# Ten background items and the sums of h, dealt out anew over five w3 steps of an fp32 Fourier-mixing and MLP kernel

## The chip, the cores and the metric

One core of one Trainium2 chip runs the whole program in one launch. The metric is device time in microseconds, as a median of runs; lower is better. Engines are named as in the profile: PE (TensorE's matmuls), PEld (its weight loads), DVE (VectorE), ACT (ScalarE), POOL (GpSimd) and SP (SyncE, which issues every DMA of the stage told of here). Each engine works through its own instructions in the order in which the program issues them and waits for the other engines by semaphores.

## What is computed

The input is one sequence of 2048 rows with 512 features, all fp32. Two layers follow each other, and each has two sublayers, both with a residual:

```
x = x + real(DFT_seq(DFT_hidden(layernorm(x))))
x = x + B(layernorm(x))
B(x): h  = gelu(layernorm(x) @ w1), its four column groups shifted by +1, -1, +2, -2 rows
      x1 = x + shifted(h) @ w2
      return x1 + gelu(layernorm(x1) @ w3) @ w4        # 512 -> 1376 -> 512
```

The case is about the last line, the MLP with w3 and w4, in the second layer (layer 1 of 0 and 1).

## The kernel before

Every fp32 matrix product is made of three matmuls on fp32r parts (`mm3`, lines 294 to 296): a tile is split into a high part (a cast, mostly on ACT) and a low part (the difference, on DVE), and the products high*high, high*low and low*high are summed in PSUM. The rows are cut into four chunks of 512 (c = 0 to 3), a chunk into four tiles of 128 rows (q = 0 to 3).

The MLP takes two chunks at a time, a pair, and multiplies them block by block by Strassen's scheme with seven products in place of eight. In layer 1, pair 0 (chunks 0 and 1) is done by `first_pair` (line 1226) and pair 1 (chunks 2 and 3) by `last_pair`. Pair 0 runs while the layer norms of chunks 2 and 3 are still open, and does them beside its own work: it normalises and turns (transposes) them into z and writes z to DRAM (`z3d[2]`, `z3d[3]`), from where pair 1's blocks are read back.

`first_pair` has three parts.

1. Two products with the last block of w3 (`w4r[0]`), whose results go through gelu into `hm0` and `hm1`.
2. Five w3 steps, `p` = 0 to 4 (line 1330 on), which this text calls the first to the fifth. A step makes seven products (`prod`, six matmuls of 512 columns each) into five PSUM banks out of a round of eight. ACT copies the first (`u`, line 1356), DVE adds up the others (`v`, `x`, `y`, all through `add`, line 480), ACT takes gelus into the step's tiles `11`, `21`, `22`, `t3` (the `hn` tiles). The sixth product goes to a bank of its own; the fifth and the seventh add to the banks of the first and the fourth (`new=False`), so the fifth waits until ACT has copied `u`, and the seventh until DVE has added `y`.
3. Thirty-nine multiplications by blocks of w4 (`multiply`), each of 12 matmuls of 256 columns, with weights in seven tiles `un0` to `un6` that are loaded in a ring (`load`, line 1281) and lie where `w3b[1]` lay, the w3 blocks of the second and fourth steps. So the first seven loads can go when the fourth step's products are done. They are issued in the fifth step, after its second product.

Three kinds of work are dealt out between the products of the w3 steps.

- `bg` is a list of ten items (`z3_steps`, line 1027), taken one by one by `one()`. Counted from 0, they are: 0 and 1, the low parts of blocks `t3` and `t4`; 2, statistics of two tiles of chunk 3 (DVE, POOL) and the norm of two tiles of chunk 2 (ACT); 3, the same for the other two; 4, DVE turns two tiles of chunk 2 into `z3turned`; 5, it turns the other two, and SP issues four DMAs that write `z3d[2]` (`turn_out`, line 614); 6 and 7, DVE adds two tiles of chunk 3 to `xs`, and ACT norms them; 8 and 9, as 4 and 5, for chunk 3 and `z3d[3]`.
- `t_sum(k, i)`: four DVE sums (Strassen's sums of h) for each step k, with i from 0 to 3; the sums of steps 0 to 3 are dealt out over steps 1 to 4 by the table `sums` and, within a step, over its four points `then(0)` to `then(3)`. `then(1)` stands between the additions `x` and `y`; `then(2)` and `then(3)` stand after the fifth and the sixth product's gelu; an item that is taken at a point follows the point's sums.
- `bring(a, b)` (line 1353): SP reads blocks a to b of the w3 step two steps on, in three pieces, after the fourth, sixth and seventh product.

Items are taken at three kinds of places: after the first and after the head products and in the first step's beginning (items 0 and 1), at points of a step by the condition in `then`, and at the end of the first three steps (`if p < 3: one()`, after `bring(3, 4)`).

In the fifth step `then` also splits the first tiles for part 3 (`high_at` on ACT, `low_at` on DVE), and the four loads `b12f`, `b11f`, `b21f`, `b22f` (line 707) read z of chunks 2 and 3 back; three of them stand in SP's queue behind the seven `un` loads, the fourth after the second multiplication.

Of the kernel before, what the change touches and what calls it, by code (L numbers as in the profile page):

```python
# [43 lines left out]
def spectral_mlp_kernel(ctx: ExitStack, tc: tile.TileContext, x, ws, hs, w1, w2, w34, out):  # L44
# [105 lines left out]
    def piece(src, a=0, b=2):  # L150
        pieces.append((src, a, b))
        return len(pieces) - 1
# [9 lines left out]
    for layer in range(LAYERS):  # L162
        for c in range(NC):
# [5 lines left out]
            for k in range(NP):  # L169
# [4 lines left out]
                p = piece(ws[c, k][:, 2:4])  # L174
# [18 lines left out]
    raws, slots, sums = {}, {}, {}  # L193
# [285 lines left out]
    def add(o, a, b, op=ALU.add):  # L479
        nc.vector.tensor_tensor(o, a, b, op=op)  # L480
# [145 lines left out]
    def gelu(g, ps):  # L626
        order = "p (q b j) -> p b q j", "p (b q j) -> p b q j"
        g_of, ps_of = (v.rearrange(o, b=NB, q=TC) for v, o in zip((g, ps), order))
        nc.scalar.activation(g_of, ps_of, AF.Gelu_apprx_tanh)
# [83 lines left out]
    def prod(o, w, u, b, new=True):  # L713
        for d in range(2):
            v = slice(d * P, (d + 1) * P)
            mm3(o, w[:, 0, u, v], w[:, 1, u, v], blk[b][:, d, 0], blk[b][:, d, 1], new and d == 0, d == 1, not new)
# [7 lines left out]
    def by_pairs(layer, zs, xin, dst):  # L724
# [347 lines left out]
        for pair in range(n_pairs):  # L1072
            c1, c2 = 2 * pair, 2 * pair + 1
            if last_of(layer):
                if pair == n_pairs - 1:
                    last_pair(c1, c2, dst, lambda: w4r[0])
                    continue
                loads = [next_block(*b) for b in ((3, 0, "12"), (2, 0, "11"), (2, 1, "21"), (3, 1, "22"))]
                first_pair(c1, c2, dst, z3_steps, loads, next_parts, w3_load, w3e_load)
                continue  # L1080
# [145 lines left out]
    def first_pair(c1, c2, dst, z3_steps, loads, next_parts, w3_load, w3e_load):  # L1226
# [15 lines left out]
        def one():  # L1242
            if bg:
                bg.pop(0)()

        def t_sum(k, i):
            f = {n: v[1] for n, v in parts[k].items()}
            o, a, b = (("t1", "t3", "11"), ("t3", "22", "t3"), ("t2", "22", "t1"), ("t4", "21", "t2"))[i]
            add(f[o], f[a], f[b], ALU.subtract)
# [29 lines left out]
        def load(n):  # L1279
            if n < len(steps):  # L1280
                nc.sync.dma_start(units[n % len(units)].bitcast(F32), steps[n][2])
# [4 lines left out]
        def high_at(i):  # L1286
            if i < len(ring):
                k, n = steps[ring[i]][1]
                act(hi_of(ring[i]), parts[k][n][1])

        def low_at(i):
            if i < len(ring):
                k, n = steps[ring[i]][1]
                lo, src = parts[k][n]
                nc.vector.tensor_tensor(lo, src, hi_of(ring[i]).bitcast(F32), op=ALU.subtract)
# [18 lines left out]
        for i, pair_of in enumerate((("11", "21"), ("12", "22"))):  # L1314
            s = w4r[0]
            for d in range(KD):
                b = blk[pair_of[d // 2]]
# [8 lines left out]
        u, v = (at(f"uv{i}", TMP + (4 + i) * CH, CH, dtype=F32) for i in range(2))  # L1326
        x, y = rest[4:6]
        sums = [(k, i) for k in range(nk - 1) for i in range(4)]
        sums = {p: sums[a:b] for p, a, b in ((1, 0, 2), (2, 2, 6), (3, 6, 12), (4, 12, 16))}
        for p in range(nk):  # L1330
            w = w3b[p % 2]
            b1, b6, b7, b5, b4 = (banks[(2 + 5 * p + i) % 8] for i in range(5))
            f = {n: t[1] for n, t in parts[p].items()}
            last = p == nk - 1

            todo = sums.get(p, [])

            def then(i):
                for k, n in todo[len(todo) * i // 4 : len(todo) * (i + 1) // 4]:
                    t_sum(k, n)  # L1340
                if last:
                    high_at(i)
                    if i:
                        low_at(i - 1)
                elif p and i > (0, 1, 1, 2)[p]:
                    one()

            def gelu_to(n, ps):
                gelu(f[n], ps)

            def bring(*v):
                if p + 2 < nk:
                    nc.sync.dma_start(w[:, :, slice(*v)].bitcast(F32), w3d[p + 2][:, :, slice(*v)])

            prod(b1, w, 4, "11")
            act(u, b1)
            prod(b6, w, 1, "t2")
            add(v, u, b6)
            if not p:
                one()  # L1360
            then(0)
            if last:
                for n in range(len(units)):
                    load(n)
            prod(b7, w, 2, "t3")
            add(x, v, b7)
            then(1)
            prod(b5, w, 0, "t1")
            bring(0, 3)
            add(y, x, b5)  # L1370
            gelu_to("22", y)
            prod(b1, w, 5, "21", new=False)
            gelu_to("11", b1)
            then(2)
            if last:
                for f_ in loads[:2]:
                    f_()
            prod(b4, w, 6, "t4")
            bring(4, 7)
            add(x, x, b4)  # L1380
            gelu_to("21", x)
            then(3)
            if last:
                loads[2]()
            prod(b5, w, 3, "22", new=False)
            add(v, v, b5)
            gelu_to("t3", v)
            bring(3, 4)
            if p < 3:
                one()  # L1390
# [6 lines left out]
        for n in range(len(steps)):  # L1397
# [4 lines left out]
            if 10 <= n < 31 and n % 3 == 1:  # L1402
                i = (n - 10) // 3
# [528 lines left out]
```

## Time and profile before

| | |
|---|---|
| median of 3 runs | 1425.03 us (1424.76 to 1426.95) |
| the profiled execution's own time | 1425.46 us |
| its span, first to last instruction | 1423.4 us |
| PE busy | 1416.0 us (99%) |
| DVE busy | 1187.3 us (83%) |
| ACT busy | 741.2 us (52%) |
| granted clock of TensorE | 1.000 |

The span leaves 2.06 us of the profiled execution's time outside. Times in timelines count from the span's start. A row of a timeline gives start, duration, engine, line, operation, out<-in, shapes and count; a bracket at its end gives the engine's idle time before it and what ended it.

The five w3 steps of `first_pair` begin on PE at 1207.23, 1216.75, 1226.27, 1235.79 and 1245.31 us, 9.52 us each, and its part 3 lies after them, up to about 1313 us.

### The profile page before, as it was taken

What the parts mean: (1) busy time and instruction counts of PE and PEld (TensorE: products, weight loads), DVE (VectorE), ACT (ScalarE), POOL (GpSimd) and SP (SyncE); (2) the same over time, 40 slices, a digit from 0 to 9 for tenths busy, and PEclk for the clock granted to TensorE, in tenths of its full rate; (3) what the DMA queues carried; (4) which work ended last, traced back from release to release, by engine and by line L of the source; (5) the groups of instructions that cost most, each with busy time, mean ns of one, the idle gap of its engine ahead of it and who ended that gap; (6) DMA issues with size and microseconds to landing.
All of it is one profiled execution on the core that took longest, in us unless ns stands there. A gap on an engine that the chain in (4) does not pass through costs nothing.

```text
span 1423.4 us, 17862 instructions
## 1 busy us (share of the span) xinstructions
PE 1416.0 (99%) x6465; PEld 1181.6 (83%) x6465; DVE 1187.3 (83%) x1675; ACT 741.2 (52%) x1007; POOL 77.2 (5%) x105
## 2 busy tenths in 40 slices
PE   9999999999999999999999999999999999999998
PEld 8888888888888888888888888888888888889887
DVE  7986998988979888656789989889899788886676
ACT  6663464455565744434555544545455666453351
POOL 2100000000002000000000000000000010000000
PEclk9999999999999999999999999999999999999999
DMA  7867647658754857944556476575686456686864
GB/s 253 279 207 236 208 154 259 194 164 308 238 163 113 287 199 266 354 156 178 203 170 218 160 252 209 163 262 167 207 297 224 134 149 231 185 257 228 311 207 158
DMA packets 136488, 306.31 MB, mean 215 GB/s; under 512 B 9680, under 2 KB 58064, under 8 KB 133712
## 3 DMA queue, kind: packets, MB, share of 16 engines
q1 hardware_dynamic: 136400, 305.17, 64.4%
q8 instruction: 51, 0.84, 0.2%
q14 instruction: 37, 0.30, 0.1%
HBM read 250.87 MB, written 54.26 MB: 214 GB/s over the span
## 4 chain that ended last, share of the span: by engine, by line
PE 99%; DMA 1%; DVE 0%; issue 0%; POOL 0%; DVEq 0%; POOLq 0%
PE psd L294 10%; PE psd L296 10%; PE psd L295 10%; PE psa L296 8%; PE psa L295 8%; PE psa L294 8%; PE psc L295 7%; PE psc L294 7%; PE psb L294 7%; PE psc L296 7%; PE psb L296 7%; PE psb L295 7%; DMA un<-w4d 1%; PE psd L139 0%; PE psb L426 0%; PE psa L426 0%
## 5 line engine op out<-in xcount | busy, mean ns | idle before, releaser
L240 ACT CAST ring<-raw 128x1024 fp32r<-128x1024 f32 x127 | 133.0, 1052 | 80.6 <-PE psd L296 43.2
L257 DVE TENSOR_TENSOR ring<-raw,ring 128x1024 fp32r<-128x1024 f32 x126 | 153.5, 1220 | 13.1 <-ACT ring L240 12.9
L294 PE MATMUL psd<-ring,rr 128*128 128x512 f32 x208 | 80.9, 389 | 0.0
L295 PE MATMUL psd<-ring,rr 128*128 128x512 f32 x208 | 80.9, 389 | 0.0
L296 PE MATMUL psd<-ring,rr 128*128 128x512 f32 x208 | 80.9, 389 | 0.0
L334 POOL TENSOR_TENSOR rs<-ve,mhalf 128x4 f32<-128x4 f32 x16 | 26.9, 1683 | 723.9 <-DVE nm L333 723.9
L247 ACT CAST ring<-ring0f 128x1024 fp32r<-128x1024 f32 x28 | 29.5, 1054 | 50.8 <-DVE ring0f L246 50.8
L257 DVE TENSOR_TENSOR ring<-ring1f,ring 128x512 fp32r<-128x512 f32 (+1 forms) x56 | 53.3, 951 | 0.7 <-ACT ring L243 0.7
L313 POOL TENSOR_TENSOR rs<-ve,mhalf 128x2 f32<-128x2 f32 (+2 forms) x33 | 28.8, 871 | 421.0 <-DVE nb L312 402.0
L342 ACT ACTIVATE tmp<-xs,nb,rs 128x512 f32<-128x512 f32 x56 | 43.3, 810 | 14.4 <-POOL nb L314 14.4
L294 PE MATMUL psc<-ring,ay 128*128 128x512 f32 x128 | 49.8, 389 | 0.0
L295 PE MATMUL psc<-ring,ay 128*128 128x512 f32 x128 | 49.8, 389 | 0.0
L296 PE MATMUL psc<-ring,ay 128*128 128x512 f32 x128 | 49.8, 389 | 0.0
L294 PE MATMUL psb<-ring,ay 128*128 128x512 f32 x128 | 49.8, 389 | 0.0
L295 PE MATMUL psb<-ring,ay 128*128 128x512 f32 x128 | 49.8, 389 | 0.0
L296 PE MATMUL psb<-ring,ay 128*128 128x512 f32 x128 | 49.8, 389 | 0.0
L294 PE MATMUL psa<-ring,ay 128*128 128x512 f32 x126 | 49.0, 389 | 0.0
L295 PE MATMUL psa<-ring,ay 128*128 128x512 f32 x126 | 49.0, 389 | 0.0
L296 PE MATMUL psa<-ring,ay 128*128 128x512 f32 x126 | 49.0, 389 | 0.0
L294 PE MATMUL psd<-ring,ay 128*128 128x512 f32 x126 | 49.0, 389 | 0.0
L295 PE MATMUL psd<-ring,ay 128*128 128x512 f32 x126 | 49.0, 389 | 0.0
L296 PE MATMUL psd<-ring,ay 128*128 128x512 f32 x126 | 49.0, 389 | 0.0
(826 smaller groups left out, 4494.0 us busy)
## 6 DMA issues: line engine op xcount, KB each, us to landing
raw<-in_ws SPq DMA_DIRECT2D x183, 512.0 KB, 5.2
raw<-in_hs SPq DMA_DIRECT2D x56, 512.0 KB, 3.6
w4r<-w4d SPq DMA_DIRECT2D x44, 512.0 KB, 4.7
w3b<-w3d SPq DMA_DIRECT2D x10, 1792.0 KB, 9.2
w3d<-w3b SPq DMA_DIRECT2D x5, 1792.0 KB, 6.9
x1d<-tmp SPq DMA_DIRECT2D x12, 512.0 KB, 6.1
xs<-x1d SPq DMA_DIRECT2D x12, 512.0 KB, 5.3
w4d<-w4in SPq DMA_DIRECT2D x11, 512.0 KB, 4.7
```

Source lines behind the costliest of these rows:

```text
L240: nc.scalar.copy(dest[:, a:b, 0], r[0][:, a:b])
L247: nc.scalar.copy(dest[:, :, 0], lo)
L257: nc.vector.tensor_tensor(lo, src, hi.bitcast(F32), op=ALU.subtract)
L294: nc.tensor.matmul(o, lh, rh, start=first, stop=False, skip_group_check=more)
L295: nc.tensor.matmul(o, lh, rl, start=False, stop=False, skip_group_check=more)
L296: nc.tensor.matmul(o, ll, rh, start=False, stop=last, skip_group_check=more)
L313: nc.gpsimd.tensor_tensor(rs[:, :n], ve[:, :n], mhalf[:, 0, :n], op=ALU.pow)
L334: nc.gpsimd.tensor_tensor(rs, ve, mhalf[:, :, :2], op=ALU.pow)
L342: nc.scalar.activation(o, s, AF.Identity, bias=mr[2], scale=mr[1])
```

## The change

Two lines of `first_pair` are changed.

```diff
-        sums = {p: sums[a:b] for p, a, b in ((1, 0, 2), (2, 2, 6), (3, 6, 12), (4, 12, 16))}
+        sums = {p: sums[a:b] for p, a, b in ((1, 0, 2), (2, 2, 4), (3, 4, 12), (4, 12, 16))}
...
-                elif p and i > (0, 1, 1, 2)[p]:
+                elif i > (2, 1, 1, 3)[p]:
                     one()
```

By the second line the first step takes an item at `then(3)`, and the fourth takes none. The count stays ten: one after the head products, then 3, 3, 3 and 0 in the first four steps where it was 2, 3, 3 and 1. Every item from 2 on moves up by one place:

| item | before | after |
|---|---|---|
| 2 (statistics, norms) | end of the first step | first step, `then(3)` |
| 3 (statistics, norms) | second step, `then(2)` | end of the first step |
| 4 (turn) | second step, `then(3)` | second step, `then(2)` |
| 5 (turn, write `z3d[2]`) | end of the second step | second step, `then(3)` |
| 6 (add, norms) | third step, `then(2)` | end of the second step |
| 7 (add, norms) | third step, `then(3)` | third step, `then(2)` |
| 8 (turn) | end of the third step | third step, `then(3)` |
| 9 (turn, write `z3d[3]`) | fourth step, `then(3)` | end of the third step |

By the first line the third step takes two of the sums of h in place of four, (0, 2) at `then(1)` and (0, 3) at `then(3)`, and the fourth step eight in place of six, two at each point. No instruction is added or removed.

## The prediction

> **What bounds the kernel now.** I read the page's first part, then the chain of work that ended last and PE's waits over the whole run, and then the stage of the change, engine by engine in order of time. The page:
>
> ```profile
> span 1423.4 us, 17862 instructions
> PE 1416.0 (99%) x6465; PEld 1181.6 (83%) x6465; DVE 1187.3 (83%) x1675; ACT 741.2 (52%) x1007; POOL 77.2 (5%) x105
> ```
>
> PE is the bound, so only PE's gaps can be won. The waits of PE (line, releaser, us in total, times, longest):
>
> ```profile
> PE psd L294 <- DMA un<-w4d: 1.6, 1, 1.6
> PE psd L139 <- POOL mhalf L55: 1.4, 1, 1.4
> PE psb L294 <- DMA un<-w4d: 0.6, 1, 0.6
> ```
>
> There are three in the whole run. L139 is the warm-up at the kernel's start; the other two are loads of w4 into `un`, in the stage right behind the five w3 steps. PE's rows there, and the windows of the fourth step, of the stage's start and of its rest (length, PE busy, PEld, DVE, ACT, POOL, clock, DMA share, GB/s):
>
> ```profile
> 1243.95 0.39 PE L294 MATMUL psd<-b,w3b 128*128 128x512 f32 x1
> 1254.60 0.39 PE L296 MATMUL psc<-b,w3b 128*128 128x512 f32 x1
> 1255.59 0.36 PE L294 MATMUL psb<-un,hr 128*128 128x256 f32 x1 [0.60 <-DMA un<-w4d]
> 1265.57 0.28 PE L296 MATMUL psa<-un,hn 128*128 128x256 f32 x1
> 1267.43 0.36 PE L294 MATMUL psd<-un,hr 128*128 128x256 f32 x1 [1.58 <-DMA un<-w4d]
> 1235.80:1245.30 9.50, 9.50 (x43) 7.87 (x42) 9.24 (x16) 5.18 (x9) 0.00 (x0) 1.00 0.57 189
> 1254.80:1269.00 14.20, 12.02 (x98) 11.69 (x98) 11.63 (x18) 8.20 (x15) 0.00 (x0) 1.00 0.96 331
> 1269.00:1311.00 42.00, 42.00 (x356) 42.00 (x356) 32.41 (x44) 19.23 (x28) 0.00 (x0) 1.00 0.72 232
> ```
>
> The five steps run without a gap, and so does the stage from 1269 on; 14.20 - 12.02 = 2.18 us of PE's time is idle between. By starts it is a little more, since a matmul's row (0.39 or 0.28) overlaps its successor. A step of 42 matmuls takes 9.52 us (front table), 0.227 a matmul, so 1254.60 should be followed at 1254.83 and was at 1255.59: 0.76. The 84 small matmuls from 1255.59 end with the one at 1265.57, so (1265.57 - 1255.59)/83 = 0.12 apart; the next was due at 1265.69 and came at 1267.43: 1.74. Together 2.50 us. That sum is what can be won.
>
> Why the loads are late is in SP's order (start, duration, DMA, how many), the chain's two DMA pieces (issue to landing), and the DVE row that SP waits for:
>
> ```profile
> 1229.84 3.11 SPq L614 DMA_DIRECT2D z3d<-z3turned  x4
> 1247.41 3.10 SPq L614 DMA_DIRECT2D z3d<-z3turned  x4
> 1250.61 5.77 SPq L1281 DMA_DIRECT2D un<-w4d  x7
> 1256.48 0.55 SPq L707 DMA_DIRECT2D b12f<-z3d  x1
> 1258.42 2.04 SPq L1281 DMA_DIRECT2D un<-w4d  x2
> 1250.61 4.85 DMA un<-w4d
> 1258.42 8.88 DMA un<-w4d
> 1246.08 1.30 DVE L604 STREAM_TRANSPOSE z3turned<-rest 128x512 f32<-128x512 f32 x2
> ```
>
> Item 9's turns end at 1247.38; its four writes hold SP until 1250.51; only then go the seven first loads, though their tiles were free when the fourth step's products ended at 1245.31 (plus 0.2, the lag of other readers behind PE here). They take 5.77, and three z loads come next, so that the eighth `un` load, due when the first multiplication is done, goes at 1258.42 into a DMA system at 0.96 and lands 8.88 later: the second gap. Both gaps have the same root, item 9's place.
>
> **The change part by part: the loads.** Item 9 moves from the fourth step to the end of the third. Below I work out its turns to end near 1239.6, so SP's four writes (3.10) are over at about 1242.7 and nothing stands before the loads at 1245.5. They go 1250.61 - 1245.5 = 5.1 us sooner. The first lands at 1245.5 + 4.85 = 1250.4; PE wants it at 1254.83, 4.4 us of slack: the 0.76 goes. The seventh is issued by 1245.5 + 5.77 = 1251.3, the three z loads follow by about 1253.3 (1256.48 to 1258.42 took 1.94), and SP is idle when the first multiplication ends: at 1254.83 + 12 x 0.12 = 1256.27. The eighth load goes at 1256.4 and is wanted at 1254.83 + 84 x 0.12 = 1264.9, 8.5 later. Its landing lies between 4.85 (the first load's, on a quiet queue) and 8.88 (behind 1.5 MB of z in flight); the z is now out 3 us before it, so I take about 5.5; at the upper end 0.4 of the 1.74 would stay.
>
> **DMAs moved past.** Item 5 goes from the second step's end to `then(3)`, ahead of `bring(3, 4)`. Its writes wait for the turns (near 1227.9 below, 1229.84 before), so that piece of w3 goes near 1231 in place of 1226.5 (0.2 behind the second step's last product). It is read by the fourth step's seventh product at 1243.95: 13 us on, free. The third step's pieces no longer stand behind the 1229.84 writes. `z3turned` is filled again by item 8, once the writes have landed:
>
> ```profile
> DMA to landing us min/median/max: 2.7/4.6/4.8
> ```
>
> The last write is issued near 1230.3 and has landed by 1235.1; item 8 comes at 1236.4. Slack 1.3.
>
> **DVE's and ACT's order.** Work comes earlier, into steps where the products wait for `u` (before the fifth) and `y` (before the seventh). I follow DVE from the second step on; these are its rows and ACT's:
>
> ```profile
> 1219.95 0.59 ACT L1356 COPY uv<-psa 128x512 f32<-128x512 f32 x1
> 1220.57 0.69 DVE L480 TENSOR_TENSOR uv<-uv,psc 128x512 f32<-128x512 f32 x1 [1.18 <-ACT uv L1356]
> 1221.36 0.69 DVE L480 TENSOR_TENSOR rest<-uv,psc 128x512 f32<-128x512 f32 x1
> 1226.32 1.30 DVE L604 STREAM_TRANSPOSE z3turned<-tmp 128x512 f32<-128x512 f32 x2
> 1227.75 0.69 DVE L480 TENSOR_TENSOR uv<-uv,psb 128x512 f32<-128x512 f32 x1
> 1230.49 0.69 DVE L480 TENSOR_TENSOR uv<-uv,psd 128x512 f32<-128x512 f32 x1 [0.71 <-ACT uv L1356]
> 1231.09 0.68 DVE L480 TENSOR_TENSOR hn4f<-hn5f,hn3f 128x512 f32<-128x512 f32 x1
> 1237.28 1.52 ACT L342 ACTIVATE rest<-rest,nb,rs 128x512 f32<-128x512 f32 x2 [0.36 <-DVE xs L480]
> 1239.82 0.69 DVE L480 TENSOR_TENSOR uv<-uv,psb 128x512 f32<-128x512 f32 x1 [0.22 <-ACT uv L1356]
> 1242.83 0.68 DVE L480 TENSOR_TENSOR rest<-rest,psd 128x512 f32<-128x512 f32 x1
> 1244.75 0.69 DVE L480 TENSOR_TENSOR hn18f<-hn19f,hn17f 128x512 f32<-128x512 f32 x1
> 1245.47 0.69 DVE L480 TENSOR_TENSOR hn20f<-hn15f,hn18f 128x512 f32<-128x512 f32 x1
> ```
>
> An addition costs 0.60 from start to start (1230.49 to 1231.09), 0.72 to 0.79 when it needs the one just before it (1244.75 to 1245.47, 1220.57 to 1221.36), a pair of turns up to 1.43 (1226.32 to 1227.75), a pair of norms 1.52. In the first step, item 2 now lies ahead of `t3`'s gelu and item 3's norms ahead of `u`, which puts the second step's `u` about 0.7 later and its `v` at 1221.27. From there: x 0.79, a sum and y 0.60 each, y done at 1223.95 (wanted at the seventh product, 1224.91); then turns 1.43, addition and sum 0.60 each, turns 1.43, and the second step's last addition near 1227.95 (before: 1227.75). Item 6 follows: the second tile is added by 1229.85, ACT's norms run 1229.25 to 1230.77, and `u` is copied by 1231.36, 0.35 before the fifth product wants it (1226.27 + 4 x 1.36 = 1231.71). So v 1231.4, x 1232.15, sum, y 1233.35 to 1234.04; wanted 1234.43: 0.4 of slack. Item 7's two additions, one more and a sum reach 1236.4; turns (item 8) 1.3, the last addition, turns (item 9) to 1239.6. In the fourth step v 1239.56, two sums, x, two sums of which the second needs the first, y at 1243.28, done 1243.97: before, y was at 1242.83, one sum earlier. The seventh product wants it at 1243.95. The slack is gone, and with the readers' lag I charge 0.1 us, between 0 and 0.4 (my steps are good to about 0.3). After y, DVE is again where it was: its fifth-step order is the same, and item 9 no longer stands between the last sum and the last addition (1247.31 before, near 1247.0 now).
>
> Against this chain speaks a rule of the Trainium skill, in VectorE: DVE Perf Modes, section The DRAIN you can't avoid: after an operation the next does not start until the pipe has emptied. By it the additions would follow at their full duration; the rows above have 0.60 between starts where one lasts 0.69, so here the rule doesn't hold for most of them, as the page's own remark on operations that are not held allows.
>
> **Sum.** 2.50 - 0.1 = 2.4 us. Against the profiled execution's own 1425.46 (2.06 outside the span) that is 1423.06; that execution lies 0.43 above the median, and for a median of runs I take 1425.03 - 2.4 = 1422.6. Nothing later eats it: PE has no other wait, and the later loads are issued by PE's own progress.
>
> **Rivals.** (1) Only the first gap closes: the eighth load still takes 8.88 or more. At 8.88 it is 0.4 late, with z loads still queued ahead of it up to the whole 1.74: 1423.0 to 1424.3. Against it: SP's 3 us of lead over the earlier order. (2) DVE becomes the bound. If each of the nineteen additions that I counted at 0.60 between v at 1221.27 and the fourth step's y costs its full 0.69, y comes 19 x 0.09 = 1.7 later, the seventh product waits 1.7 + 0.1, and most of the gain is given back: 1425.03 - 2.50 + 1.8 = 1424.3. For it: DVE is busy 9.24 of 9.50 in that step already; against it: the 0.60 in every row. (3) Slower: item 8 must wait for item 5's writes, ahead of which SP now also has two `bring` pieces in flight. DVE's additions stand behind that turn, in order. The wait starts to count at a landing of 6.1 us (1236.4 - 1230.3), and what exceeds it PE pays in the fourth step; past 8.5 the whole gain is gone, and at 11.5 the kernel is 3 us slower, 1428. For it: an `un` load took 8.88 under load; against it: these writes took at most 4.8. (4) More than the gaps: 0.36 in place of 0.28 for the first matmul behind each wait, and other small losses at the restart, would add 0.2 to 0.6: 1422.0 to 1422.4.
>
> **How the numbers follow.** Forecast 0.66, rival 1 0.09, rival 2 0.07, rival 3 0.08, rival 4 0.10. About 0.2% (2.85 us, down to 1422.18) is what a measurement of this kernel can tell from no change, and my 2.4 lies inside it, 0.4 from its edge; medians move by that much (the three runs span 2.2 us). So I give faster by over 0.2% 0.4 of the forecast's cases (0.26) and nearly all of rival 4 (0.09): 0.35; slower the better part of rival 3: 0.06; within: 0.59. The range 1421.6 to 1424.6 holds the forecast's cases, most of rival 4, rival 1 and the middle of rival 2, and leaves out rival 3 and the far ends.
>
> **What would show it.** Right: no wait of PE on `un`; the seven loads start on SP near 1245.5, the `z3d[3]` writes near 1239.6; the windows after the third part 2.4 us earlier; y of the fourth step near 1243.3. Wrong: a wait of PE on `uv` or `rest` in the third or fourth step (rival 2), of DVE's turns on a DMA (rival 3), or a wait on `un` left at the eighth multiplication (rival 1).

## The result and the profile after

The changed kernel takes 1423.12 us in the median of 16 runs (1422.96 to 1423.51), the one before 1425.20 (1424.57 to 1427.13): a ratio of 0.9984, 95% interval 0.9976 to 0.9991. That is 2.08 us, or 0.15%; the forecast was 2.4, in the range 1421.6 to 1424.6. The profiled execution took 1423.03, its span 1421.1.

PE's waits in the changed kernel, over the whole run:

```profile
PE psd L139 <- POOL mhalf L55: 1.4, 1, 1.4
PE psb L426 <- DVE rr L339: 0.2, 1, 0.2
```

Both waits on `un` are gone; the second row here lies in another part of the kernel. SP in order of time, two windows of the stage (columns as in the prediction), and the DVE row of item 9's turns:

```profile
1228.13 3.10 SPq L614 DMA_DIRECT2D z3d<-z3turned  x4
1239.68 3.55 SPq L614 DMA_DIRECT2D z3d<-z3turned  x4
1245.91 4.45 SPq L1281 DMA_DIRECT2D un<-w4d  x7
1250.46 0.55 SPq L707 DMA_DIRECT2D b12f<-z3d  x1
1256.86 1.94 SPq L1281 DMA_DIRECT2D un<-w4d  x2
1235.80:1245.30 9.50, 9.43 (x42) 7.48 (x41) 9.40 (x16) 3.76 (x7) 0.00 (x0) 1.00 0.94 292
1254.80:1266.50 11.70, 11.70 (x98) 11.62 (x97) 11.02 (x18) 7.91 (x14) 0.00 (x0) 1.00 0.91 298
1238.36 1.29 DVE L604 STREAM_TRANSPOSE z3turned<-rest 128x512 f32<-128x512 f32 x2
```

Item 9's turns end at 1239.65, its four writes hold SP until 1243.23, and the seven loads go at 1245.91, 4.7 us sooner than before. The stage behind the steps is without a gap (11.70 of 11.70). But the steps themselves, which had none, now have two small ones, which the list of waits does not show. They show in PE's starts, 0.23 apart elsewhere (the last two rows are the first and the eighth multiplication):

```profile
1231.25 0.39 PE L296 MATMUL psa<-bt,w3b 128*128 128x512 f32 x1
1231.59 0.50 PE L294 MATMUL psd<-b,w3b 128*128 128x512 f32 x1
1231.93 0.39 PE L295 MATMUL psd<-b,w3b 128*128 128x512 f32 x1
1243.76 0.39 PE L296 MATMUL psd<-bt,w3b 128*128 128x512 f32 x1
1244.22 0.50 PE L294 MATMUL psd<-b,w3b 128*128 128x512 f32 x1
1244.55 0.39 PE L295 MATMUL psd<-b,w3b 128*128 128x512 f32 x1
1255.24 0.29 PE L294 MATMUL psb<-un,hr 128*128 128x256 f32 x1
1265.20 0.28 PE L294 MATMUL psd<-un,hr 128*128 128x256 f32 x1
```

At the third step's fifth product two intervals of 0.34 stand where 0.227 is due (0.22 lost), at the fourth step's seventh 0.46 and 0.33 (0.34 lost). The steps begin at 1206.98, 1216.50, 1226.04, 1235.83 and 1245.71, so the third and the fourth take 9.79 and 9.88 in place of 9.52: 0.10 more is spread over intervals too near 0.227 to be told apart. So the account of the stage is this. From the first step's first matmul (1207.23 before, 1206.98 after) to the first multiplication it took 48.36 and takes 48.26: the first gap of 0.76 went and 0.66 was lost in the steps. From there to the eighth multiplication it took 11.84 and takes 9.96: 1.88 won. Together 1.98, and the medians say 2.08.

### The profile page after: what moved, and what is told of

Its sections match the earlier page's. It is cut to its first block, busy times and chain, and to the rows that moved or that the text cites. A ratio compares the mean times of both kernels' runs of the same rounds, so it can differ in the third digit from the quotient of the medians.

```text
span 1421.1 us, 17861 instructions
## 1 busy us (share of the span) xinstructions
PE 1415.4 (100%) x6465; PEld 1180.1 (83%) x6465; DVE 1187.0 (84%) x1675; ACT 743.0 (52%) x1007; POOL 77.7 (5%) x105
## 4 chain that ended last, share of the span: by engine, by line
PE 93%; DVE 4%; ACT 1%; issue 1%; POOL 0%; DMA 0%; DVEq 0%; ACTq 0%; POOLq 0%
PE psd L294 10%; PE psd L296 10%; PE psd L295 9%; PE psa L296 8%; PE psa L294 8%; PE psa L295 8%; PE psb L296 7%; PE psc L295 7%; PE psc L296 7%; PE psb L294 7%; PE psb L295 7%; PE psc L294 7%; DVE rest L480 0%; ACT tmp L342 0%; DVE ring L257 0%
```

## The experiments

The theory was: item 9's place made both gaps, because its writes stand ahead of the `un` loads in SP's queue; DVE's fuller order then costs PE a little in the steps. The rivals were that the early items as a whole or the move of the sums gain by themselves, that the second gap is not from the z loads, and that the small waits are DVE's load alone. All medians are of 11 runs, and ratios are to the kernel before on the same chip, with 95% intervals.

**Items alone.**

```diff
 before, with
-                elif p and i > (0, 1, 1, 2)[p]:
+                elif i > (2, 1, 1, 3)[p]:
```

> The ten items are moved as in the change, the sums of h stay where they were (four in the third step, six in the fourth). Theory (item 9's place in SP's queue made both gaps): the un loads start near 1245.9, no wait of PE on un; but one more sum stands ahead of y in the third step and two more in all in that step, so y comes about 0.6 us later in the third and in the fourth step than in the changed kernel, and PE loses 0.4 to 0.7 more before its seventh products: 1423.5 to 1423.9, 0.9989 of before. Rival (the sums' move is what gains): within 0.3 us of before, 1425.2.

1423.12, ratio 0.9986 (0.9977 to 0.9995): as the full change, and 0.4 below the expected range. Both gaps on `un` are gone. PE's starts show 0.17 lost at the third step's fifth product, and 0.38 at that step's seventh, where y came late as expected; but the fourth step lost only 0.11 at its seventh, since that product was then due later too. Delays of one chain don't add: what the third step has lost, the fourth needn't lose again.

**Sums alone.**

```diff
 before, with
-        ... ((1, 0, 2), (2, 2, 6), (3, 6, 12), (4, 12, 16))}
+        ... ((1, 0, 2), (2, 2, 4), (3, 4, 12), (4, 12, 16))}
```

> Only the table of sums is changed (two in the third step, eight in the fourth), the items stay. Theory: item 9's turns still end near 1247.4, the un loads still start near 1250.6, both gaps stay: 1425.2 within 0.3 us. Rival (the sums' move is what gains): 1423 to 1424.

1425.94, ratio 1.0008 (0.9999 to 1.0016): no gain, and 0.4 above what was expected. PE's waits, and SP:

```profile
PE psd L294 <- DMA un<-w4d: 1.9, 1, 1.9
PE psb L294 <- DMA un<-w4d: 1.0, 1, 1.0
1247.82 3.10 SPq L614 DMA_DIRECT2D z3d<-z3turned  x4
1251.02 5.84 SPq L1281 DMA_DIRECT2D un<-w4d  x7
```

With two sums more ahead of it in the fourth step, item 9 comes 0.4 later than before, and both gaps grow; PE's starts show 0.29 more lost at the fifth step's seventh product. The sums' move is not the gain; without the items' move the trace has more idle time than before, though the interval of the ratio just holds 1.

**Item 9 alone.**

```diff
 before, with
-                elif p and i > (0, 1, 1, 2)[p]:
+                elif p and i > (0, 1, 1, 3)[p]:
...
             if p < 3:
                 one()
+            if p == 2:
+                one()
```

> Of the items only number 9 is moved: it is taken with item 8 at the end of the third step; the others and the sums stay. Theory: SP is free before 1245.5, both gaps go (2.5 us); DVE has 1.3 us of turns more ahead of the fourth step's additions, so y there comes about 1 us later than before and PE waits 0.5 to 0.8 at the seventh product: 1423.2 to 1423.6. Rival (all items' earlier places are needed): gain under 1 us, above 1424.2.

1423.12, ratio 0.9985 (0.9976 to 0.9994). One item moved by one place gives all of it. PE now has a listed wait in the fourth step:

```profile
1244.19 0.50 PE L294 MATMUL psd<-b,w3b 128*128 128x512 f32 x1 [0.30 <-DVE rest L480]
1245.90 4.49 SPq L1281 DMA_DIRECT2D un<-w4d  x7
```

That is y, behind 2.5 us of turns in one piece; by starts PE loses 0.58 there. The moves of items 2 to 8 and of the sums win nothing on top: they trade this wait for the two smaller ones.

**SP held by other writes.** The changed kernel, with four writes of `u` to tiles in DRAM that nothing reads (`hold`), ahead of the loads (its added line moves all later line numbers up by one or more):

```diff
 the changed kernel, with
+    hold = [dram.tile([P, CH], F32, name=f"hold{i}") for i in range(4)]
...
             if last:
+                for i in range(4):
+                    nc.sync.dma_start(hold[i], u)
                 for n in range(len(units)):
                     load(n)
```

> The changed kernel, with four writes of 256 KB to unused DRAM in SP's queue ahead of the seven un loads; they carry u, which ACT copies in the fifth step by 1249.2. Nothing else is touched, the items stay early. Theory (SP's order alone makes both gaps): the writes hold SP until about 1252.3, the first un load lands near 1257.2 where PE wants it at 1255.2 (gap 2.0), the z loads and the eighth un load follow 1.7 later than before the change, the eighth lands near 1269 where PE wants it at 1267.3 (gap 1.5 to 2): 1426.4 to 1427.4. Rival (the early turns and sums gain by themselves): at most 1424.

1424.15, ratio 0.9993 (0.9984 to 1.0002): 1.03 over the changed kernel, and 2.2 below the expected range. The mechanism held and two sizes were off: four plain writes took SP 1.82 us, not 3.1, and the first load landed 3.6 after its issue, not 4.85. So it landed at 1254.75, in time, and only the second gap came back:

```profile
1249.24 1.82 SPq L1365 DMA_DIRECT2D hold<-uv  x4
1251.15 4.46 SPq L1282 DMA_DIRECT2D un<-w4d  x7
1257.75 8.39 DMA un<-w4d
1266.28 0.36 PE L295 MATMUL psd<-un,hr 128*128 128x256 f32 x1 [0.86 <-DMA un<-w4d]
```

By starts (1265.13 to 1266.28, 0.12 due) it is 1.03, the whole difference. The same with eight writes:

> As sp_hold (the changed kernel with writes of u ahead of the un loads), with eight writes in place of four; in sp_hold four took SP only 1.82 us, the first un load landed 3.6 after its issue and made no gap, and the eighth load made one of 1.0. Theory (SP's order makes both gaps, by the time at which the loads go): eight writes hold SP from 1249.2 to about 1252.9, the first un load lands at 1256.5 to 1257.7 where PE wants it at 1255.2, the first gap is back with 1.3 to 2.5, the second with 0.5 to 1.5: 1425.3 to 1426.5. Rival (the first gap is not from SP's order): the first gap stays away, 1424.2 to 1424.8.

1426.94, ratio 1.0008 (0.9999 to 1.0018), 3.8 over the changed kernel and 0.4 above the expected range; 0.3 of that may be the chip, whose median of the kernel before is 1425.51 where it was 1425.20 in the result. By starts the two gaps are 2.52 and 1.00. SP was held until 1253.44, and both gaps are back though every item is early:

```profile
1249.41 4.03 SPq L1365 DMA_DIRECT2D hold<-uv  x8
1253.54 4.54 SPq L1282 DMA_DIRECT2D un<-w4d  x7
1255.24 0.39 PE L297 MATMUL psc<-b,w3b 128*128 128x512 f32 x1
1257.99 0.36 PE L295 MATMUL psb<-un,hr 128*128 128x256 f32 x1 [2.37 <-ACT hr L1290]
1269.02 0.36 PE L295 MATMUL psd<-un,hr 128*128 128x256 f32 x1 [0.84 <-DMA un<-w4d]
```

The wait of 2.37 is put down to ACT here, but the first load was issued at 1253.54 and its landing is listed as 4.3 later, at 1257.84, just ahead of PE's start. PE wanted it at 1255.47. With the landing of the changed kernel (3.1) it would have come at 1256.64, by estimate, so the late issue alone makes about half of this gap; the slower landing, behind the 2 MB that the added writes move, makes the rest. What stands ahead of the loads on SP makes the gaps, then, and not the place of the items as such.

**The z loads later.** The kernel before, with the four z loads behind the third to sixth multiplication:

```diff
-            if last:
-                for f_ in loads[:2]:
-                    f_()
...
-            if last:
-                loads[2]()
...
-            if n == 1:
-                loads[3]()
+            if 2 <= n <= 5:
+                loads[n - 2]()
```

> The kernel before the change, with the four z loads taken out of the fifth step and issued one by one after the third to the sixth multiplication, so that the eighth un load has no z load ahead of it; items and sums as before. Theory (the second gap is the eighth load behind 1.5 MB of z): the first gap stays (0.76), the eighth load goes near 1257.1, lands in 4.9 to 6 us, 1265.7 is not missed, the second gap (1.74) goes: 1423.3 to 1423.7, unless DVE's sums of z, which then wait about 2 us longer, hold up the low parts. Rival (the load is slow by itself): 1425.2.

1424.98, ratio 0.9999 (0.9990 to 1.0008): missed. The second gap did go: with no z ahead of it the eighth load went at 1257.33 and landed in 4.6, where it took 8.88. But two later waits took the gap's place:

```profile
PE psc L294 <- ACT hr L1289: 1.1, 1, 1.1
PE psb L294 <- ACT hn29f L629: 0.6, 1, 0.6
PE psc L294 <- DMA un<-w4s: 0.2, 1, 0.2
1269.12 1.23 DVE L480 TENSOR_TENSOR bt1f<-b12f,b11f 128x1024 f32<-128x1024 f32 x1 [5.12 <-DMA b11f<-z3d]
```

The middle row is the first gap: the first load landed 4.9 after 1250.62, just before PE started at 1255.64. The profile names ACT's gelu instead; but in the kernel before that gelu ended at 1255.74, after PE had started at 1255.59, so it is not what PE waits for. The proviso of the expectation came true: DVE stood 5.12 us in its sum of z, with the low parts queued behind. By starts PE loses 0.80, 0.32 (at 1274.54) and 1.26 (at 1287.49), 2.38 in all for the 2.50 of before; that the last one comes from DVE's wait is argued from the order of DVE's queue, not tested. So the second gap was the eighth load behind the z loads, and moving those back to these places doesn't pay.

**The two small waits.** In the changed kernel DVE's addition into v at the end of the first step waits for ACT's norms of chunk 2, which don't touch v:

```profile
1218.14 0.69 DVE L480 TENSOR_TENSOR uv<-uv,psd 128x512 f32<-128x512 f32 x1 [0.36 <-ACT tmp L342]
```

`u` and `v` lie in the last two sixths of the tile `tmp`, the norms write the first four. The next kernel gives them memory of their own in the first four steps:

```diff
 the changed kernel, with
-        u, v = (at(f"uv{i}", TMP + (4 + i) * CH, CH, dtype=F32) for i in range(2))
+        uv = [[at(f"uv{i}{j}", w + i * CH, CH, dtype=F32) for i in range(2)] for j, w in enumerate((D_, TMP + 4 * CH))]
...
+            u, v = uv[last]
```

> The changed kernel, with u and v of the first four steps in memory of their own in place of the tail of the tile tmp, which the norms and turns of chunk 2 use. Theory (instructions on different parts of tmp are made to wait for each other): DVE's addition into v at the end of the first step no longer waits for ACT's norms (0.36 us idle at 1218.14 in the changed kernel), u of the third step is copied about 0.4 us earlier, PE's wait at the third step's fifth product (0.22 us) goes and that at the fourth step's seventh (0.34 us) shrinks to 0.0 to 0.3: 1422.6 to 1422.9. Rival (the waits come from DVE's load alone): as the changed kernel, 1423.1.

1422.29 (1421.97 to 1422.70), ratio 0.9978 (0.9969 to 0.9987): 0.3 below the expected range, and below every run of the changed kernel. The same addition starts without a wait, the second step's v comes at 1220.94 (1221.78 in the changed kernel), and the third step's v, at 1231.57 there, comes 0.93 earlier:

```profile
1217.68 0.68 DVE L480 TENSOR_TENSOR uv<-uv,psd 128x512 f32<-128x512 f32 x1
1220.94 0.69 DVE L480 TENSOR_TENSOR uv<-uv,psc 128x512 f32<-128x512 f32 x1 [0.82 <-ACT uv L1357]
1230.64 0.69 DVE L480 TENSOR_TENSOR uv<-uv,psd 128x512 f32<-128x512 f32 x1 [1.52 <-ACT uv L1357]
```

The five steps take 47.61 us, from 1206.96 to the first multiplication at 1254.57, five times 9.52: both small waits are gone. The same edit on the kernel before:

> The kernel before the change with u and v of the first four steps in memory of their own, as in uv_apart. Theory: ACT's wait for the turns ahead of the third step's u (0.76 us at 1229.86) goes, and since PE didn't wait there and item 9 keeps its place, both gaps on un stay: 1425.2 within 0.4, un loads from about 1250.5. Rival (the tile's place gains by itself what uv_apart gained, 0.8): 1424.4.

1425.26, ratio 1.0003 (0.9994 to 1.0011). No gain, as expected: PE did not wait for those additions there. Its trace has the waits on `un` in three pieces, 0.37, 0.48 and 1.40 by starts, 2.25 in all. Last, the sums dealt six and six over the fourth and fifth step, on the changed kernel and on `uv_apart`:

```diff
-        ... ((1, 0, 2), (2, 2, 4), (3, 4, 12), (4, 12, 16))}
+        ... ((1, 0, 2), (2, 2, 4), (3, 4, 10), (4, 10, 16))}
```

> The changed kernel with six sums of h in the fourth step and six in the fifth in place of eight and four; u and v stay where they were. Theory (DVE's chain to y in the fourth step is one sum too long): y comes 0.6 us earlier, PE's wait at the fourth step's seventh product (0.34 us) goes, that at the third step's fifth product (0.22, ahead of which nothing changes) stays: 1422.7 to 1422.9. Rival (the two waits have one cause, the late u of the third step): both stay, 1423.1.

1422.78, ratio 0.9978 (0.9969 to 0.9987), as expected. Its runs (1422.29 to 1423.22) overlap those of the changed kernel, so what follows rests on the trace. The fourth step's wait is gone: y starts at 1243.12, 35.62 after the first step's first matmul (1207.50 in that execution) where the changed kernel has 36.50 (1243.48 - 1206.98), and DVE afterwards waits for PE (0.28 at 1244.69) instead of PE for DVE. The third step's two intervals of 0.34 stay. So the third step's wait comes from the late `u` alone. The fourth step's needs both the lateness and the eighth sum: it goes with this edit, and it goes with `uv_apart`, which keeps the eight sums.

> uv_apart, with six sums of h in the fourth step and six in the fifth in place of eight and four. y of the fourth step comes 0.6 us earlier, that of the fifth 0.6 later (still 0.5 ahead of its product). Theory: uv_apart has no wait of PE left in this stage, so nothing more is to be won: 1422.3 within 0.3. Rival (short waits under the profile's resolution remain): 1421.9 or less.

1422.39, ratio 0.9979 (0.9970 to 0.9988), as `uv_apart`: nothing was left to win.

## Why the prediction was right, and where it was off

**The loads: right.** SP's order made both gaps: loads at 1245.91 (forecast 1245.5), item 9's turns ended at 1239.65 (1239.6), no wait on `un` is left, and a hold of SP by eight added writes brings both gaps back with every item still early. The eighth load landed 3.6 us after 1256.86 (I took 5.5), at 1260.46, 4.7 before it was wanted at 1265.20. The first landed in 3.1, where I took 4.85. Both loads had more slack than I gave them. The eighth load's size and landing, from the list of DMAs:

```profile
un<-w4d SPq DMA_DIRECT2D x1, 256.0 KB, 3.6
```

The second gap was worth 1.88 rather than 1.74: the slow first matmul behind each wait (0.36), which I had left to rival 4, belongs to it.

**The steps: right in kind, too small.** I charged 0.1 us for y in the fourth step, between 0 and 0.4, and PE lost 0.66 in the steps. The term that was mis-sized is the second step's `u` and `v`. I put v at 1221.27; it came at 1221.78, in a stage that began 0.25 sooner, so 0.76 late by the steps' clock. From there the 0.35 of slack that I gave the third step's `u` was gone (0.22 lost), and y in the fourth step ended 37.18 after the first step's first matmul instead of 36.74 (0.34 lost). The rows of v and y in the changed kernel:

```profile
1221.78 0.69 DVE L480 TENSOR_TENSOR uv<-uv,psc 128x512 f32<-128x512 f32 x1 [1.19 <-ACT uv L1356]
1243.48 0.68 DVE L480 TENSOR_TENSOR rest<-rest,psd 128x512 f32<-128x512 f32 x1
```

What I had not put in are the waits through `tmp`. Taking them away (`uv_apart`) puts the second step's v 13.98 after the first step's first matmul, where I had 14.04 and the changed kernel has 14.80, and makes all five steps gapless. The trace of before held the clue, in the third step's `u`, of whose wait I had quoted only the echo on DVE (0.71 at 1230.49):

```profile
1229.86 0.59 ACT L1356 COPY uv<-psd 128x512 f32<-128x512 f32 x1 [0.76 <-DVE z3turned L604]
```

This copy waited until DVE's turns, which read `tmp`, were done; no operand of it explains that. I followed the order of the queues and the operands, not that row's releaser.

**DMAs moved past: right.** No wait of DVE on a DMA in these steps: DVE's turns (item 8) began at 1236.57 with the chunk 2 writes landed. `bring(3, 4)` behind item 5's writes cost nothing.

**The rivals.** The eighth load (1) was in time. DVE (2) became the bound, for 0.66 and not for 1.8: additions still follow 0.60 apart (1233.57 to 1234.17 in the changed kernel). (3) did not come. (4) is real, 0.14, but the steps' loss covers it. By the trace the sum is 0.76 + 1.88 - 0.66 = 1.98, for a forecast of 2.50 - 0.1. That the total came so near owes a little to luck: the gaps were worth 0.14 more than I took and the steps lost 0.56 more than I charged.

## What to carry to other kernels

When a load is late, look first at what stands ahead of it on its issuing queue and at what that waits for: here four transposed writes of one item, issued one place too late, cost 2 us through the loads behind them, and moving that single item gave all that the change gave. Before filling an engine's order more tightly, read the releasers of its present waits and find those that no operand explains: here tiles cut from one buffer waited for each other, and where the slack was a few tenths of a microsecond PE paid for it. And count a delay along one chain once: what one step has lost, the next needn't lose again.

## What was not expected of the hardware

The time in which SP is held by a DMA, and the landing, differed with what was moved and with what stood ahead. Four writes of 256 KB from the turned tile held SP 3.10 to 3.55 us, four plain writes of the same size 1.82. The seven `un` loads, the same in all kernels, held it 5.77 us right behind the turned writes, but 4.45 on a quiet queue and 4.46 right behind the four plain writes. The first of them landed after 4.85, 3.1 and 3.6 us in these three cases. No run here shows why. A hold estimated from one pattern was wrong by 1.3 us for another.
